# Forward table by a signed permutation on TensorE, last input part ahead of the inverse table, first filter copies on VectorE in finer parts

## The chip, the cores and the metric

The kernel runs on one core of one Trainium2 chip. The metric is the time of an execution on the device, in microseconds; lower is better. Each kernel was executed several times.

Engines are named as in the profile: PE is TensorE, PEld its weight loads, DVE is VectorE, ACT is ScalarE, POOL is GpSimd. The span runs from the first to the last instruction of the profiled execution; the device time of the same execution is about 2 us longer (792.0 against 793.8). An eviction is the copy by which another engine takes a matmul's result out of the bank that TensorE wrote it to, so that the bank is free again.

## The reference

The program filters a sequence in the frequency domain and applies a two-layer network with a Gelu to the result. Cut to what matters:

```
x: (8, 3008, 256)   filt_r, filt_i: (1505, 256)   w_in: (256, 2048)   w_out: (2048, 256)

X = rfft(x, axis=1)
y = irfft(X * (filt_r + 1j * filt_i), n=3008, axis=1)      # per batch and channel
h = y.reshape(24064, 256) @ w_in
out = (0.5 * h * (1 + erf(h / sqrt(2)))) @ w_out
```

## The kernel before

The transform of length 3008 = 47 x 64 is done by matmuls with tables in two steps each way. The tables are not read from memory: they are computed in the kernel (angles on VectorE, sines on ScalarE). Batch 0 runs ahead of the network in a stretch of its own; batches 1 to 7 are woven into the network's loop. Only the stretch of batch 0 is touched by the change. The second step works on 24 blocks, counted by `k`; each of its twelve products covers two of them. Its parts are:

- `c1`: 16 pieces of the first step on the input `x_sb`, evicted to `at_sb`.
- `table_2_angle`, `table_2_sin`: the forward table `T2` of the second step. `table_3`: the inverse table `T3`, which is `T2` transposed (24 transposes on TensorE). `table_4`: a small last table.
- `c1t`: transposes of `at_sb`. `c2`: the second step and the product with the filters `F`. `c3`, `c3t`, `c4`: the way back.
- `dup_filters`: partitions 64 to 127 of `F` are a copy of partitions 0 to 63.

```
    def dup_filters(self, eng, k0, k, ts=(0, 1)):
        for t in ts:
            o, i = (self.F[r:r + 64, t, k0:k0 + k, :].rearrange("p a b -> p (a b)") for r in (64, 0))
            ...
                eng.tensor_copy(out=o, in_=i)
    ...
    def table_2_sin(self, k0, k):
        act, t2 = self.nc.scalar.activation, self.T2[:, k0:k0 + k]
        w, r = self.gen[:, 0, k0:k0 + k], self.gen[:, 1, k0:k0 + k]
        act(out=t2[:, :, 1, :], in_=w, func=AF.Sin, scale=2.0 * PI)
        act(out=t2[:, :, 2, 0:32], in_=r[:, :, 0:32], func=AF.Sin, scale=-2.0 * PI, bias=self.hp)
        act(out=t2[:, :, 2, 32:64], in_=r[:, :, 32:64], func=AF.Sin, scale=2.0 * PI, bias=self.hm)
    ...
    for k, n in ((0, 4), (4, 6), (10, 6), (16, 8)):
        m.load_filters(k, n)
    m.load_w_in()
    for k, n in ((4, 6), (10, 6), (16, 4), (20, 4)):
        m.dup_filters(nc.gpsimd, k, n)

    for u in range(16):
        m.c1(u // 2, u % 2, False if 4 <= u < 8 or u % 2 and u > 7 else act)
        if u == 3:
            m.table_2_sin(0, 12)
        if u == 7:
            m.table_2_sin(12, 12)
            nc.scalar.activation(out=warm, in_=m.p, func=AF.Gelu)       # loads the Gelu table
            ...                                                         # T2[0] = -T2[2]; small copies T1p, T1q
        if u == 11:
            m.table_4()
            for q in range(3):
                m.table_3(q, act if q % 2 else False)
    ...
    m.c1t(0, False)
    m.c1t(1, act)
    m.dup_filters(nc.vector, 0, 4)
    for q in range(7):
        if q < 6:
            m.c2(2 * q)
            if q + 2 < 6:
                m.c1t(q + 2, act)
            m.c2(2 * q + 1)
        if q >= 1:
            m.c3(q - 1)
```

## Time and profile before

| | before |
|---|---|
| median time, us | 791.95 (790.87 to 792.96, 3 runs) |
| span of the profiled execution, us | 792.0 |
| PE busy over the span | 762.1 us, 96% |
| first `ps_h` matmul (first of the network's loop) | 50.17 us |
| first product `p` on VectorE | 25.42 us |

The busy share of PE is an average over two very different stretches. From the first `ps_h` matmul on, PE is busy nearly all the time. Before it (32.25 of the first 50 us busy), batch 0 is brought through a chain in which every engine waits for another in turn. The useful number for this change is therefore the start of the first `ps_h` matmul: everything ahead of it is what the change touches. The prediction shows the lines of this stretch and how to read them.

### The profile page before, as it was taken

The numbers are of one execution on the slowest core, as the hardware profiler recorded it, in microseconds if no ns is written. First come the engines' busy times: TensorE is split into PE (matmuls) and PEld (weight loads), VectorE is DVE, ScalarE is ACT, GpSimd is POOL, SyncE is SP. The second block draws the span as 40 slices with busy tenths as digits, with TensorE's granted clock in tenths as the row PEclk, the third lists the DMA queues.
The fourth block names the chain that finished last, engine by engine and source line by source line (L and its number), as shares of the span: only waits on it lengthen the run. The fifth ranks groups of instructions, "written<-read, shape, count | busy, mean of one in ns | idle before, by whom it ended". The sixth has DMA issues, their size and how long they took to land.

```text
span 792.0 us, 14572 instructions
## 1 busy us (share of the span) xinstructions
PE 762.1 (96%) x5817; PEld 539.9 (68%) x5914; DVE 411.2 (52%) x725; ACT 565.6 (71%) x963; POOL 64.7 (8%) x154
## 2 busy tenths in 40 slices
PE   4789999999999999999999999999999999999997
PEld 3666766677676767667677676666767777666666
DVE  7984756466464645646455564546645366421011
ACT  5578965798557885588755887569865688566663
POOL 8700200011000200002000020001100000000000
PEclk9999999999999999999999999999999999999999
DMA  9854862555435553446614566154642521501111
GB/s 142 152 93 131 159 159 67 147 119 112 115 84 156 104 133 84 111 138 130 144 50 107 146 123 157 38 162 107 124 130 63 164 76 60 133 28 40 41 41 54
DMA packets 86341, 85.64 MB, mean 108 GB/s; under 512 B 5824, under 2 KB 76480, under 8 KB 86272
## 3 DMA queue, kind: packets, MB, share of 16 engines
q1 hardware_dynamic: 77760, 68.70, 30.7%
q0 software_dynamic: 8512, 16.00, 14.2%
q8 instruction: 46, 0.75, 0.4%
q14 instruction: 23, 0.19, 0.1%
HBM read 54.00 MB, written 46.66 MB: 127 GB/s over the span
## 4 chain that ended last, share of the span: by engine, by line
PE 90%; DMA 3%; DVE 3%; ACT 1%; issue 1%; POOL 0%; SPq 0%; DVEq 0%; POOLq 0%
PE ps_o L436 40%; PE ps_h L422 37%; PE ps_s L240 3%; PE ps_s L313 3%; DMA d_sb<-R 3%; PE ps_s L263 2%; PE ps_s L288 2%; ACT y_sb L225 1%; PE ps_c L351 1%; PE ps_c L367 1%; DVE p L354 0%; DMA b_sb<-R 0%; DVE at_sb L227 0%; PE ps_t L216 0%; DVE F L99 0%
## 5 line engine op out<-in xcount | busy, mean ns | idle before, releaser
L425 ACT ACTIVATE g_sb<-ps_h 128x512 bf16<-128x512 f32 x752 | 439.2, 596 | 191.0 <-PE ps_h L422 163.2
L436 PE MATMUL ps_o<-w_out_sb,g_sb 128*128 128x256 bf16 x3008 | 449.1, 272 | 3.0
L422 PE MATMUL ps_h<-y_sb,w_in_sb 128*128 128x512 bf16 (+2 forms) x1503 | 426.6, 365 | 0.7 <-ACT y_sb L225 0.7
L436 PEld LDWEIGHTS <-g_sb 128*128 128x128 bf16 x3008 | 287.6, 98 | 133.8
L422 PEld LDWEIGHTS <-w_in_sb 128*128 128x128 bf16 x1600 | 155.0, 98 | 23.4 <-issue 0.9
L440 DVE COPY ost<-ps_o 128x512 f32<-128x512 f32 x94 | 64.3, 684 | 125.2 <-PE ps_o L436 124.7
L271 DVE TENSOR_TENSOR p<-ps_s,F 128x512 bf16<-128x512 f32 x84 | 58.1, 691 | 103.7 <-ACT p L270 97.1
L229 DVE TENSOR_SCALAR y_sb<-ps_s 128x376 bf16<-128x376 f32 x112 | 61.0, 548 | 83.5 <-PE ps_s L313 83.5
L227 DVE CAST a_sb<-ps_s 96x512 bf16<-96x512 f32 x112 | 76.3, 686 | 41.3 <-PE ps_s L240 41.2
L227 DVE CAST v_sb<-ps_s 128x512 bf16<-128x512 f32 x84 | 57.6, 686 | 13.0 <-PE ps_s L288 13.0
L269 ACT ACTIVATE p<-ps_s 64x512 bf16<-64x512 f32 x84 | 49.8, 593 | 2.0
L313 PEld LDWEIGHTS <-d_sb 96*128 96x128 bf16 x448 | 30.3, 97 | 29.7 <-DMA d_sb<-R 3.8
L270 ACT CAST p<-ps_s 64x512 bf16<-64x512 f32 x84 | 48.5, 577 | 1.0
L104 POOL COPY gate<-p 1x1 bf16<-1x1 bf16 x48 | 8.5, 177 | 490.1 <-DVE p L273 490.1
L240 PE MATMUL ps_s<-x_sb,T 94*96 94x512 bf16 x112 | 42.7, 381 | 0.5
L313 PE MATMUL ps_s<-T,d_sb 96*128 96x94 bf16 x448 | 36.3, 204 | 3.9 <-DMA d_sb<-R 2.7
L273 DVE TENSOR_TENSOR p<-p 128x512 bf16<-128x512 bf16 x84 | 35.7, 425 | 2.9
L272 DVE TENSOR_TENSOR p<-p,F 128x512 bf16<-128x512 bf16 x84 | 34.9, 415 | 0.0
L82 POOL DMA_DIRECT2D x_sb<-in_x_dram x64 | 32.5, 510 | 13.0 <-issue 11.0
L263 PE MATMUL ps_s<-b_sb,T 128*128 128x256 bf16 x168 | 32.1, 273 | 0.4
L288 PE MATMUL ps_s<-p,T 128*128 128x256 bf16 x168 | 32.1, 273 | 0.2
L288 PEld LDWEIGHTS <-T 128*128 128x128 bf16 x168 | 16.4, 98 | 20.0 <-DVE p L273 0.5
(91 smaller groups left out, 193.0 us busy)
## 6 DMA issues: line engine op xcount, KB each, us to landing
out_dram<-ost SPq DMA_DIRECT2D x94, 256.0 KB, 2.5
x_sb<-in_x_dram POOLq DMA_DIRECT2D x64, 188.0 KB, 3.9
R<-a_sb SPq DMA_DIRECT2D x56, 192.0 KB, 3.0
b_sb<-R SPq DMA_DIRECT2D x28, 384.0 KB, 4.3
R<-v_sb SPq DMA_DIRECT2D x42, 256.0 KB, 4.0
d_sb<-R SPq DMA_DIRECT2D x56, 192.0 KB, 4.5
w_in_sb<-in_moe_w_in_dram POOLq DMA_DIRECT2D x2, 512.0 KB, 8.7
w_out_sb<-in_moe_w_out_dram POOLq DMA_DIRECT2D x2, 512.0 KB, 10.9
```

Of the source, the lines that this page charges most:

```text
L227: self.nc.vector.tensor_copy(out=out, in_=in_)
L229: self.nc.vector.tensor_scalar(out=out, in0=in_, scalar1=scale, scalar2=None, op0=ALU.mult)
L240: nc.tensor.matmul(ps[0:96, :], lhsT=self.T1, rhs=self.st[b, "x"][:, 2 * u:2 * u + 2, :], start=True, stop=True)
L269: nc.scalar.activation(out=p2[0:64], in_=ps[64:128], func=AF.Copy, scale=-1.0)
L270: nc.scalar.copy(out=p2[64:128], in_=ps[0:64])
L271: nc.vector.tensor_tensor(out=p1, in0=ps, in1=f(0), op=ALU.mult)
L288: nc.tensor.matmul(ps[:, 256 * i:256 * i + 256], lhsT=self.T3[:, k].rearrange("p a b -> p (a b)"), rhs=w[:, 256 * i:256 * i + 256], start= ...
L313: nc.tensor.matmul(ps[:, 94 * i:94 * i + 94], lhsT=d[:, (grp % 2) * 4 + i, 128 * half:128 * half + 128], rhs=t4, start=True, stop=True)
L422: nc.tensor.matmul(ps[:, o:o + n], lhsT=self.w_in_sb[:, dc, jc * 128:jc * 128 + 128], rhs=self.ring[:, dc, off:off + n], start=(dc == 0), ...
L425: nc.scalar.activation(out=self.st["g", t][:, jc, :], in_=ps, func=AF.Gelu)
L436: nc.tensor.matmul(ps[:, tile_i % 2, :], lhsT=g[:, jc, tile_i * 128:tile_i * 128 + 128], rhs=self.w_out_sb[:, jc, :], start=(jc == 0), sto ...
L440: nc.vector.tensor_copy(out=ost, in_=ps)
```

## The change

The intent is to shorten the stretch before the first `ps_h` matmul in three ways, each meant to take work off VectorE's path:

1. **Rotated table.** The cosine part of `T2` is the sine part with pairs of rows exchanged and a sign. The change computes only sines and makes the rest by a matmul with a signed permutation matrix (`swap`), evicted by ScalarE. The second half's angles start from the first half's.
2. **Input ahead of the inverse table.** Only one third of `T3` is transposed before the last input part; the other two go into the product loop. `table_4` moves near the end of it, its small copies to GpSimd, its weights into a hole at the start. Evictions are shared out anew between VectorE and ScalarE, the Gelu table load moves into the product loop, and `c3` reads a product's tile in another order.
3. **Filter copies.** VectorE copies the first six `k` in three pieces of two `k` (both parts together) in place of four `k` in two pieces. GpSimd copies the next four ahead of the `w_in` load and the rest in pieces of two `k`.

The diff, cut to its core (cuts are marked with `...`):

```
-    def dup_filters(self, eng, k0, k, ts=(0, 1)):
-        for t in ts:
-            o, i = (self.F[r:r + 64, t, k0:k0 + k, :].rearrange("p a b -> p (a b)") for r in (64, 0))
...
+    def dup_filters(self, eng, k0, k):
+        for k in range(k0, k0 + k, 2):
+            o, i = (self.F[r:r + 64, :, k:k + 2, :].rearrange("p t a b -> p t (a b)") for r in (64, 0))
+            eng.tensor_copy(out=o, in_=i)
...
+        ts(out=self.swap, in0=cols, scalar1=self.to, scalar2=self.sg, op0=ALU.is_equal, op1=ALU.mult)
...
-        v.scalar_tensor_tensor(out=r, in0=w, scalar=-1.0, in1=w, op0=ALU.mult, op1=ALU.max)
...
-        act(out=t2[:, :, 2, 0:32], in_=r[:, :, 0:32], func=AF.Sin, scale=-2.0 * PI, bias=self.hp)
-        act(out=t2[:, :, 2, 32:64], in_=r[:, :, 32:64], func=AF.Sin, scale=2.0 * PI, bias=self.hm)
...
+    def table_2_swap(self, h):
+        t2 = self.T2[:, 12 * h:12 * h + 12]
+        for s, j in ((1.0, 0), (-1.0, 32)):
+            ps = self.bank("ps_sw", "n")
+            self.nc.tensor.matmul(ps[:, 0:384], lhsT=self.swap, rhs=t2[:, :, 1, j:j + 32], start=True, stop=True)
+            self._evac(t2[:, :, 2, j:j + 32], ps[:, 0:384].rearrange("p (k j) -> p k j", k=12), "act", s)
...
-    for k, n in ((0, 4), (4, 6), (10, 6), (16, 8)):
+    for k, n in ((0, 4), (4, 2), (6, 4), (10, 6), (16, 8)):
         m.load_filters(k, n)
+    m.dup_filters(nc.gpsimd, 6, 4)
     m.load_w_in()
-    for k, n in ((4, 6), (10, 6), (16, 4), (20, 4)):
-        m.dup_filters(nc.gpsimd, k, n)
+    ...                                     # T1p, T1q on GpSimd
+    m.dup_filters(nc.gpsimd, 10, 14)
...
-        m.c1(u // 2, u % 2, False if 4 <= u < 8 or u % 2 and u > 7 else act)
+        m.c1(u // 2, u % 2, act if u < 4 or u % 2 else False)
...
-            nc.scalar.activation(out=warm, in_=m.p, func=AF.Gelu)
...
         if u == 11:
-            m.table_4()
-            for q in range(3):
-                m.table_3(q, act if q % 2 else False)
+            m.table_3(0, False)
...
-    m.dup_filters(nc.vector, 0, 4)
+    m.dup_filters(nc.vector, 0, 6)
...
+        if 1 <= q < 3:
+            m.table_3(q, act)
+        if q == 3:
+            nc.scalar.activation(out=warm, in_=m.p, func=AF.Gelu)
         if q >= 1:
             m.c3(q - 1)
+        if q == 5:
+            m.table_4()
```

## The prediction

> **What bounds the kernel now.** The page puts PE at 96% busy, and ScalarE's and VectorE's shares at 71% and 52%. I asked next for the windows by stage: from 70 us on, PE is busy 29.79 of 30, 99.03 of 100, 197.13 of 200 us, so the long loop is bound by TensorE, and the diff touches nothing in it. What the diff touches lies before the first `ps_h` matmul, which the timeline has at 50.17 us. So the question is how many microseconds earlier that matmul comes; everything after is expected to shift as a block. I then read the chain that ended last, in order of time, from 5 to 27 us:
>
> ```profile
> 5.56 1.02 DVE gen L173
> ...
> 11.90 0.96 DVE gen L178
> 12.86 1.86 DVE at_sb L227 x4
> ...
> 16.34 2.73 PE ps_t L216 x24
> 19.09 1.22 DVE T L227
> 20.32 0.94 DVE at_sb L227 x2
> ...
> 22.63 2.70 DVE F L99 x2
> ...
> 25.42 1.24 DVE p L354
> ```
>
> The reader is to see that from 5.56 to 25.42 us the chain is nearly all VectorE: angles of the forward table, copies of the transformed input queued behind them, 24 transposes for the inverse table in the middle of PE's program, then two filter copies. After 25.42 the twelve products set the pace. The timeline shows this stage:
>
> ```profile
> 14.64 0.55 DVE L502 TENSOR_SCALAR T<-T 128x1536 bf16<-128x1536 bf16 x1
> 19.14 10.02 POOL L99 COPY F<-F 64x1536 bf16<-64x1536 bf16 x8
> 22.63 2.69 DVE L99 COPY F<-F 64x1024 bf16<-64x1024 bf16 x2
> 26.70 0.99 PE L351 MATMUL ps_c<-b_sb,T 128*128 128x256 bf16 x4 [2.57 <-DVE p L354]
> 27.48 1.06 PE L339 MATMUL ps_c1t<-eye,at_sb 128*128 128x128 bf16 x8
> 31.01 0.61 PE L339 MATMUL ps_c1t<-eye,at_sb 128*128 128x128 bf16 x8
> 31.21 9.14 DVE L354 TENSOR_TENSOR p<-ps_c,F 128x1024 bf16<-128x1024 f32 x8 [0.55 <-PE ps_c L351]
> ```
>
> Two things to see. The two filter copies of 1024 elements take 2.69 us together, while a larger copy-like VectorE operation (1536 elements, 128 partitions) takes 0.55: GpSimd was copying filters all that time. And PE, idle for 2.57 us before 26.70, then needs 1.06 us for eight transposes that take 0.61 at 31.01. The windows confirm the second:
>
> ```profile
> 25.00:26.00 1.00, 0.00 (x0) 1.00 1.04 209
> 27.00:28.00 1.00, 1.00 (x9) 0.50 0.07 12
> 31.00:32.00 1.00, 1.00 (x16) 1.00 1.01 184
> ```
>
> The fourth number is the granted clock: 1.00, then 0.50 after the idle stretch, 1.00 again by 31.
>
> **What the Trainium skill says.** "SBUF — State Buffer", section "Who interferes with whom": VectorE in a two-port mode and GpSimd share a port pair under an exclusive lock; the second to issue blocks for the whole instruction of the first. The trace agrees: VectorE's copies last 1.08 and 1.68 us, GpSimd's 64x1536 copies 1.34 us median with one stretched to 1.66, which is one VectorE copy (0.31 us) more. "VectorE: DVE Perf Modes", section "Side-by-side: where the cycles go for N=2048 bf16": four elements a cycle plus some 150 cycles at 0.96 GHz. For 1024 elements I estimate from this (256+150)/0.96 = 0.42 us; the same form gives 0.56 for 1536, and the trace has 0.55. "TensorE: Matmul & The Clock Gate", section "What's actually happening": half clock by default and after an idle window of about 3.4 us, full clock after a busy one. The trace agrees on the halving; its idle stretch was only 2.57 us, so here the threshold is at best approximate (the page's window is free-running).
>
> **The change part by part.** All starts below are worked from durations above and from rows of the same view.
>
> *Forward table.* Removed from VectorE: two absolute-value passes of 0.96 us, and the second half's angle starts from the first by a 0.56 us tensor-scalar in place of 1.02. Added: three one-column operations (about 0.2 us), one 128x128 mask (0.2). Removed from ScalarE: four sines of 128x384, 0.60 each. Added: four evictions of 128x384 at 0.49, and four matmuls of 384 columns, 0.5 us each at half clock. VectorE's angle work ends at about 5.76+1.02+0.58+0.98 (first half, 8.36), +0.4 (masks), +0.58+0.58+0.98 = 10.85, where it ended at 12.86. But the rotated quarter now goes sine, matmul, eviction: first sine 8.40 to 9.24, matmuls to 10.1, evictions to 10.7; second sine held behind input evictions until 11.9, done 12.76, matmuls 13.6, evictions 14.24, negation on VectorE 14.28 to 14.63. VectorE waits in that negation, so the two pieces of input meant for it go at 14.55 to 15.57. That gives back over half of the 2 us.
>
> *Input ahead of inverse tables.* In the order of PE's instructions, 8 transposes now stand before the last input part instead of 24 and two `ps_t4` matmuls: 16 x 0.107 + 0.36 = about 2.1 us off PE's stretch. One third is evicted on VectorE (1.22) at about 16.2 to 17.5; the last input part is evicted by 18.45 on both engines, where it was 21.26. The first transposes of it start at 18.5 instead of about 21.3 (-2.75 us), and VectorE reaches the filter copies at about 19.9 instead of 22.63. The other two thirds move into the product loop: 8 transposes (0.45) and a ScalarE eviction of 1.02 in each of two rounds.
>
> *Filter copies.* Three copies of 1024 instead of two. Alone: 3 x 0.33 = 1.0 us. GpSimd, however, now issues 20 filter loads instead of 16. It is held by input landings until the eighth is issued at 13.5; then 12 x 0.55 = 6.6 gives 20.1 us for its first copy. Against 19.9 for VectorE this is a close race. If VectorE wins, the first product starts at about 20.9 to 21; if it loses, each copy alternates with a 1.03 us GpSimd copy and the product starts at 23.0.
>
> *Products.* Twelve at a pace of 1.14 us (9.14 for eight), 13.7 us, plus gaps while PE catches up. In the good case PE idles only some 0.9 us before the third product's matmuls, so it keeps its clock; I count gaps of 0.2, 0.2 and 0.4 us around the rounds with the extra transposes. Last product ends 35.4 instead of 40.36: -5.0. In the bad case PE idles about 2.8 us, falls to half clock, and third to sixth product wait as they did: last end about 39.1, -1.2.
>
> *Rest.* GpSimd's later filter copies: two ready at 21.3 and 22.4, then w_in issues and two small copies, then seven from 24.0 to 31.4; product 5 needs the third at 26.9 and gets it at 25.1; product 8 has over 2 us in hand. The Gelu table load (1.28 + 0.20) moves from 14.03, where ScalarE was idle, to about 30.7, where the evictions of `vt` follow; the banks for the round after next are free again by 33.3 against a need at 33.6, so I count 0. The next input's load starts at 31.4 instead of 29.11 but is needed only after 44. The final stretch (8.1 us from 42.04 to 50.17) has the same operations. Sum: -5.0 to -1.2.
>
> **The rivals.** (a) *The copies lose the lock race*: speaks for it, that both sides come within 0.3 us by my sums; against, that a load being issued delays a copy little (the 0.55 above ran beside load issues) and the finer copies suit it. It makes 790.6. (b) *ScalarE becomes the bound of the product loop*: 1.02+1.02+2x0.55 = 3.1 us in a round with extra transposes against 2.28 for two products, plus the table load. Against: two such rounds only, three rounds of slack after. It would cost 0.5 to 1 us: 788. (c) *GpSimd's copies become the bound*: they end later than before (31.4 against 29.2) while products begin earlier. If load issues run 1.5 us longer than I count, each late product waits; 788.5. (d) *The shift is lost in the loop*, because later loads or the first DRAM round trip have less slack: loads have several us, so I give it little; then 791.
>
> **Range and chances.** I give the good case (-5, with (b) or (c) taking a little) about half, something in between (-3, one copy blocked) a quarter, the bad case (-1.3) a quarter: mean -3.6, and the three runs of before spread by 2 us. Prediction **788.2 us**, range **786.2 to 790.7**. 2% is 15.8 us; the whole stretch touched is 45 us and nothing in it can give that. Faster 0.01, same 0.985, slower 0.005.
>
> **What would show it.** First `ps_h` matmul at 45 to 49 us instead of 50.17. VectorE's angles end near 10.9; the first transposes of the whole input start near 18.5; three filter copies near 19.9, 0.3 to 0.4 us each if free and over 1 us if locked; the first product near 21 (23 if locked); granted clock 1.00 all through 20 to 30 us in the good case, 0.50 in the bad; products 1.14 us apart at the end. Wrong, if the second sine or the negation comes much later than 14.6 us, if the products wait for GpSimd, or if PE's busy share after the first `ps_h` falls.

## The result, and the profile after

The changed kernel took 789.82 us (median of 4 runs, 788.94 to 791.01) against 791.96 us of before (4 runs). The ratio is 0.9974, with a 95% interval of 0.9955 to 0.9994. Ratios are the mean time of one kernel's runs over that of the other's runs of the same rounds, so they are not quite the ratio of the medians quoted. Repeated later with more rounds, the ratio was 0.9964. By the rule of 2% it is the same time; as a small number it is 2.1 to 2.9 us faster. All outputs are right.

The first `ps_h` matmul now starts at 46.67 us, 3.50 us earlier. The chain that ended last, in order of time, in the part that was VectorE's before (start, length in us, what):

```profile
19.73 1.33 DVE F L96 x2
21.05 1.04 issue
22.10 0.42 DVE F L96
22.52 0.02 issue
22.54 0.03 DVE p L367
22.56 1.11 issue
23.68 1.23 DVE p L367
24.90 0.04 issue
24.95 0.60 PE ps_c L364 x4
25.54 0.45 PE ps_t L229 x8
25.99 0.89 PE ps_c L380 x16
```

The first product stands at 22.54 instead of 25.42. From about 25 us the chain is TensorE's: the transposes moved into the loop (`ps_t L229`) lie on it. The timeline of the same stretch:

```profile
17.93 1.89 PE L352 MATMUL ps_c1t<-eye,at_sb 128*128 128x128 bf16 x16 [0.55 <-DVE at_sb L240]
...
19.68 2.21 POOL L96 COPY F<-F 64x1024 bf16<-64x1024 bf16 x2
19.73 2.78 DVE L96 COPY F<-F 64x1024 bf16<-64x1024 bf16 x3
...
20.55 1.06 PE L352 MATMUL ps_c1t<-eye,at_sb 128*128 128x128 bf16 x8
...
23.82 0.61 PE L364 MATMUL ps_c<-b_sb,T 128*128 128x256 bf16 x4 [1.52 <-DVE p L367]
...
24.27 0.61 PE L352 MATMUL ps_c1t<-eye,at_sb 128*128 128x128 bf16 x8
...
27.82 9.14 DVE L367 TENSOR_TENSOR p<-ps_c,F 128x1024 bf16<-128x1024 f32 x8 [0.66 <-POOL F L96]
```

Three things are to be seen. GpSimd began its two filter copies at 19.68, and VectorE its three at 19.73: VectorE lost the race by 0.05 us, and its copies took 2.78 us. TensorE waited 1.52 us for the first product and was not slowed afterwards (eight transposes in 0.61 us at 24.27). But it ran at half speed before that: eight such transposes took 1.06 us at 20.55. The windows by microsecond, whose fourth number is the granted clock, do not show it:

```profile
20.00:21.00 1.00, 1.00 (x9) 1.00 0.99 140
...
25.00:26.00 1.00, 1.00 (x16) 1.00 1.08 217
...
27.00:28.00 1.00, 1.00 (x15) 1.00 1.06 213
```

The granted clock reads 1.00 at 20 us too. In the profile of early_copies (below) the same column reads 0.50 from 20 to 22 us, and eight transposes take 1.06 us there as well, so half clock is the likely reason here. In this early stretch the duration of an instruction, not that column, tells TensorE's speed.

In the last line of the timeline the wait of the fifth product is put down to a GpSimd copy. By the code this product reads `k` 8 and 9, which GpSimd's second copy fills, and that copy had ended at 21.89. What ends just before the product starts at 27.82 are TensorE's transposes (27.16 + 0.61 = 27.77). So the name is not to be trusted here; what held the product is not shown.

**After the first `ps_h` matmul.** The start was the same to 0.02 us in the two profiles of the changed kernel (46.67 and 46.69), and the time is not: it spreads by 2 us in either kernel. The waits of TensorE from 50.3 us to the end (total us, times, longest) show one source that repeats (left out is one wait of 0.7 us for ScalarE just after the start, in the kernel before). First the kernel before, then two profiles of the changed kernel:

```profile
PE ps_s L313 <- DMA d_sb<-R: 2.7, 6, 0.7
```

```profile
PE ps_s L326 <- DMA d_sb<-R: 0.6, 2, 0.3
PE ps_s L276 <- DMA b_sb<-R: 0.5, 1, 0.5
```

```profile
PE ps_s L326 <- DMA d_sb<-R: 2.1, 4, 0.6
PE ps_s L276 <- DMA b_sb<-R: 0.5, 1, 0.5
```

These are waits for the intermediate results of later batches on their way back from memory. Within one kernel they differ by 1.5 us (1.1 against 2.6), and the two spans differ by 1.1 us (787.2 and 788.3). This noise is as large as most effects studied below. So the experiments are judged by the first `ps_h` matmul, and the time is quoted beside it. This has a weakness: each kernel but the changed one has a single profile, and TensorE's speed in the start, which moves the first `ps_h`, is not the same in all of them (see early_copies and fine_unsplit).

### The profile page after: what moved, and what is told of

Same layout as the page of the kernel before. It is cut to its first block, busy times and chain, and to the rows that moved or that the text cites. A ratio compares the mean times of both kernels' runs of the same rounds, so it can differ in the third digit from the quotient of the medians.

```text
span 787.2 us, 14592 instructions
## 1 busy us (share of the span) xinstructions
PE 762.2 (97%) x5821; PEld 540.1 (69%) x5918; DVE 406.7 (52%) x720; ACT 567.4 (72%) x968; POOL 65.7 (8%) x161
## 4 chain that ended last, share of the span: by engine, by line
PE 93%; DMA 3%; issue 1%; POOL 1%; ACT 1%; DVE 1%; SPq 0%; DVEq 0%; POOLq 0%
PE ps_o L450 42%; PE ps_h L436 38%; PE ps_s L253 3%; PE ps_s L326 3%; PE ps_s L276 2%; PE ps_s L301 2%; DMA d_sb<-R 1%; DMA x_sb<-in_x_dram 1%; ACT y_sb L238 1%; PE ps_c L380 1%; POOL F L91 1%; PE ps_c L364 1%; DMA b_sb<-R 0%; POOL x_sb L82 0%; DMA F<-in_filt_i_dram 0%
## 5 line engine op out<-in xcount | busy, mean ns | idle before, releaser
L301 PEld LDWEIGHTS <-T 128*128 128x128 bf16 x168 | 16.4, 98 | 20.1 <-DVE p L286 0.5
```

The source lines that it names most:

```text
L301: nc.tensor.matmul(ps[:, 256 * i:256 * i + 256], lhsT=self.T3[:, k].rearrange("p a b -> p (a b)"), rhs=w[:, 256 * i:256 * i + 256], start= ...
```

## The experiments

Twelve runs were made, all with 5 rounds: the changed kernel again and eleven others. For each, the first `ps_h` matmul is from its one profile. The last column is span less first `ps_h` of that profile, which is the network's loop. By the rule of 2% every one of them is the same time as before. The intervals of the twelve ratios reach 0.0012 to 0.0016 to either side, about 1 us, so neighbours are not told apart by time.

| run | first product, us | first `ps_h`, us | median time, us | ratio to before | loop, us |
|---|---|---|---|---|---|
| before | 25.42 | 50.17 | 791.96 to 792.89 | 1 | 741.8 |
| after (result above) | 22.54 | 46.67 | 789.82 | 0.9974 | 740.5 |
| after_again | 22.55 | 46.69 | 789.99 | 0.9964 | 741.6 |
| early_copies | 20.97 | 45.69 | 788.18 | 0.9942 | 740.7 |
| undo_filters | 21.99 | 46.07 | 788.92 | 0.9950 | 741.7 |
| undo_table | 22.37 | 46.50 | 788.83 | 0.9951 | 741.7 |
| order_only | 20.58 | 45.25 | 787.46 | 0.9940 | 740.4 |
| undo_input | 22.86 | 46.24 | 788.84 | 0.9958 | 740.7 |
| early_warm | 20.88 | 45.59 | 787.55 | 0.9938 | 740.5 |
| before_small | 25.07 | 48.57 | 791.80 | 0.9995 | 740.7 |
| order_unsplit | 24.52 | 49.16 | 790.14 | 0.9965 | 740.2 |
| small_gelu | 24.62 | 48.11 | 790.29 | 0.9975 | 740.0 |
| order_warm | 20.61 | 45.24 | 788.15 | 0.9943 | 740.9 |
| fine_unsplit | 22.91 | 46.61 | 789.29 | 0.9966 | 741.0 |

The theory at the start was that VectorE's lost race for the ports had held the first product back, and that most of the gain comes from the order of TensorE's program. The main rivals were that the rotated table carries the gain, that TensorE's half clock bounds the stage, and that part of the gain is lost in the loop.

**after_again: the changed kernel once more.** No edit.

> The changed kernel once more, with more rounds. Both theories: first ps_h matmul at 46.7 us within 0.2, the three filter copies on VectorE about 1.25, 1.25 and 0.4 us. Theory 'the start's 3.5 us pass whole into the time': ratio to before 0.9956, about 788.5 us. Rival 'part of it is lost in the loop': ratio stays near 0.9974, and PE's busy share after the first ps_h matmul is lower than before's.

The start was the same to 0.02 us, and the ratio was 0.9964 (0.9951 to 0.9976). The mean difference is thus 0.0036 x 792.84 = 2.9 us, and the interval reaches to 3.9. The full 3.5 us is inside it, and so is a loss of over 1 us. In the first result's interval the same holds. The loop's length spreads by 1.8 us over the table, with no order by kernel that one profile each could show. Whether a little of the gain is lost in the loop stays open.

**early_copies: VectorE's filter copies moved into its wait.**

```
+    m.dup_filters(nc.vector, 0, 6)
     m.c1t(0, False)
     m.c1t(1, act)
-    m.dup_filters(nc.vector, 0, 6)
```

> The three first filter copies on VectorE stand before the first transposes' eviction, in the 1.1 us in which VectorE waited before 19.00. Theory 'the lock with GpSimd's copies delayed the first product': the copies take about 0.33 us apart between 17.9 and 19, the eviction stays at 19.0, the first product starts at about 20.8 instead of 22.54, the first ps_h matmul at about 45.0 instead of 46.7, time 1.7 us under the changed kernel's. Rival 'TensorE, still at half clock, is the bound after 19.7': first product at 20.8 too, but the gain shrinks to under 0.7 us by the first ps_h matmul. Rival 'GpSimd's later copies become the bound': products from the fourth on wait for GpSimd, same small gain.

The timeline of VectorE:

```profile
17.91 1.23 DVE L96 COPY F<-F 64x1024 bf16<-64x1024 bf16 x3
19.18 0.69 DVE L240 COPY b_sb<-ps_c1t 128x1024 bf16<-128x1024 bf16 x1
20.97 1.23 DVE L367 TENSOR_TENSOR p<-ps_c,F 128x1024 bf16<-128x1024 f32 x1 [1.10 <-PE ps_c L364]
22.68 3.48 DVE L367 TENSOR_TENSOR p<-ps_c,F 128x1024 bf16<-128x1024 f32 x3 [0.48 <-PE ps_c L364]
```

The three copies take 1.23 us together in place of 2.78, in a stretch in which GpSimd only issued filter loads. The lock theory (VectorE's copies are slow because GpSimd holds the ports that they share) holds for the first product, which is 1.57 us earlier (20.97 for 22.54). The first `ps_h` is earlier by only 1.00 us, between what the theory (1.7) and the rival of a TensorE bound (under 0.7) expected. Both waits in the lines are for TensorE (`ps_c L364`), so the rival has a part in it. At 788.18 us it is a little faster than both kernels: all of its runs lie below all of after_again's (at most 788.67 against at least 789.04).

One thing differs that the edit does not explain. The sixteen transposes of the whole input took 1.07 us here and 1.89 us in the changed kernel, and TensorE was quicker already at 15.48 us (twelve matmuls in 0.83 us against 1.17), while the first moved copy starts at 17.91. The first product did not come earlier by it: VectorE's eviction of these transposes began only when its copies were through, at 19.18 instead of 19.00.

**undo_filters: the third part undone.** The loads, GpSimd's copies and VectorE's two copies are as before; the small copies T1p and T1q stay on GpSimd.

```
-    for k, n in ((0, 4), (4, 2), (6, 4), (10, 6), (16, 8)):
+    for k, n in ((0, 4), (4, 6), (10, 6), (16, 8)):
-    m.dup_filters(nc.gpsimd, 6, 4)
-    m.dup_filters(nc.gpsimd, 10, 14)
+    for k, n in ((4, 6), (10, 6), (16, 4), (20, 4)):
+        m.dup_filters(nc.gpsimd, k, n)
-    m.dup_filters(nc.vector, 0, 6)
+    m.dup_filters(nc.vector, 0, 4)
```

> The changed kernel with the filter part undone: four loads groups, the old copies of one t each, two on VectorE. Theory 'the filter part gains nothing, since the race for the ports was lost either way': copies on VectorE together 1.6 to 2.7 us, first product at 22.0 to 22.9, first ps_h matmul within 0.4 us of 46.7. Rival 'the finer parts carry a good share': first product a microsecond later or more, first ps_h at 47.7 or later.

VectorE's two copies took 2.14 us, the first product came at 21.99, and the first `ps_h` at 46.07. The last is 0.2 us earlier than the theory's range: beside the other two parts, the filter part costs 0.60 us.

**undo_table: the first part undone.** The old sines, angles and constants are put back; the rest stays.

```
-            m.table_2_sin(0)
-            m.table_2_swap(0)
+            m.table_2_sin(0, 12)
...
-            m.table_2_minus(0)
-            m.table_2_sin(1)
-            m.table_2_swap(1)
-            m.table_2_minus(1)
+            m.table_2_sin(12, 12)
+            ...                             # T2[0] = -T2[2] for all 24 k, on VectorE
```

> The changed kernel with the forward table by sines again. Theory of the prediction, that the rotation gives back what it saves: VectorE's angles end at 12.9 instead of 10.9, but its negation comes at about 14.0 to 14.6 either way, the first transposes of the whole input at 17.9 within 0.4, first ps_h matmul 46.5 to 47.1. Rival 'the rotated table is the main source of the gain': first ps_h at 48.2 or later.

The first whole-input transposes start at 17.76 instead of 17.93, and the first `ps_h` at 46.50 instead of 46.67. The theory holds: the rotation is worth nothing here, though VectorE's angles end 2 us earlier with it (10.91 against 12.88). The reason shows in VectorE's negation, which waits for ScalarE either way (the changed kernel first, then undo_table):

```profile
14.07 0.49 DVE L199 TENSOR_SCALAR T<-T 128x768 bf16<-128x768 bf16 x1 [1.96 <-ACT T L238]
```

```profile
14.06 0.66 DVE L502 TENSOR_SCALAR T<-T 128x1536 bf16<-128x1536 bf16 x1 [0.26 <-ACT T L182]
```

The time saved on angles has become a wait: 1.96 us before the negation, where it was 0.26, and the negation starts at the same moment.

**order_only: parts one and three undone together.** What is left of the change is its second part. The edit is the two edits above.

> The changed kernel with both the rotated table and the filter part undone; what is left is the order: last input part ahead of two thirds of the inverse table, the small tables moved off VectorE, other engines for some evictions, the later table load. Theory 'the order alone carries the gain': first ps_h matmul at 45.8 to 46.4 us, at least as early as the changed kernel's 46.7; time ratio to before 0.994 to 0.996. Rival 'the three parts need one another, and undoing two of them loses what undoing one did not': first ps_h at 47.5 or later.

```profile
18.47 1.12 POOL L114 DMA_DIRECT2D w_in_sb<-in_moe_w_in_dram  x2
...
19.51 0.83 DVE L99 COPY F<-F 64x1024 bf16<-64x1024 bf16 x2
20.60 4.29 POOL L99 COPY F<-F 64x1536 bf16<-64x1536 bf16 x3
```

The first `ps_h` is at 45.25, even earlier than the theory's range, and the time is 787.46 us: 4.6 us under before, and the lowest of all. The lines of VectorE and GpSimd say why. VectorE comes to its copies at 19.51 while GpSimd is still busy with the `w_in` load and two small copies; both pieces take 0.83 us together. GpSimd's long copies start only at 20.60. The second part alone carries more than the whole gain. TensorE's half speed has a price in it too, but a limited one: the twelve products take 14.95 us from 20.58 on, against 13.67 us where they run without a gap (undo_input, below), so from the first product on it costs at most 1.28 us.

**undo_input: all of the inverse table ahead of the last input part again**, with parts one and three kept.

```
         if u == 11:
-            m.table_3(0, False)
+            for q in range(3):
+                m.table_3(q, act if q % 2 else False)
...
-        if 1 <= q < 3:
-            m.table_3(q, act)
```

> The changed kernel with all three thirds of the inverse table transposed ahead of the last input part, as in before; table 4 stays late. The prediction's step: 16 transposes at 0.107 us, 1.7 us, and their evictions return to the path, so the first transposes of the whole input start at about 19.7 instead of 17.9 and the first ps_h matmul at 48 or later. Rival 'the product loop gives it back': VectorE's filter copies then come after GpSimd's first two and run freely (0.4 us each), the first product starts at about 23 instead of 22.5, the two rounds lose 0.45 us each of transposes, and the first ps_h stays within 0.5 us of 46.7.

The transposes of the whole input start at 19.67 instead of 17.93, as the prediction's step has it, and yet the first `ps_h` comes 0.43 us earlier (46.24). The rival holds, though the copies are not free from the first: VectorE reaches them at 21.05, GpSimd's second copy ends at 21.75 (19.73 + 2.02), and VectorE's three take 1.78 us. The product loop then runs twelve products without a gap:

```profile
22.86 13.67 DVE L367 TENSOR_TENSOR p<-ps_c,F 128x1024 bf16<-128x1024 f32 x12
```

**order_unsplit: the same edit in the order-only kernel.**

> The order-only kernel with all 24 inverse-table transposes ahead of the last input part again. Beside the order-only kernel it prices the step 'last input part ahead of the inverse table' by itself. The prediction's step: 1.7 us of transposes come back to the path, first transposes of the whole input at 19.5 instead of 17.74, first ps_h matmul at 46.5 or later instead of 45.25. Rival 'the product loop gives back all of it' (as two of the rounds lose 0.45 us of transposes each, and the clock is up earlier): first ps_h within 0.4 us of 45.25.

The transposes start at 19.40 instead of 17.74, a step of 1.66 us, as expected. But the first `ps_h` comes at 49.16 instead of 45.25, 3.91 us later. The timeline:

```profile
19.66 4.48 POOL L99 COPY F<-F 64x1536 bf16<-64x1536 bf16 x3
21.22 3.20 DVE L99 COPY F<-F 64x1024 bf16<-64x1024 bf16 x2
...
25.80 0.61 PE L350 MATMUL ps_c<-b_sb,T 128*128 128x256 bf16 x4 [2.30 <-DVE p L353]
26.25 0.99 PE L338 MATMUL ps_c1t<-eye,at_sb 128*128 128x128 bf16 x8
```

VectorE arrives among GpSimd's long copies, and its two copies take 3.20 us where they took 0.83. With the 1.66 us this makes up the whole difference, which already stands at the first product (24.52 against 20.58). TensorE then waits 2.30 us, and its clock falls (0.50 granted from 27 to 28 us; the transposes at 26.25 take 0.99), as in the kernel before. That adds nothing against order_only, which had its half speed earlier: from the start of the first product to the end of the last, both take 14.9 us. By time the step is worth less than 3.91 us: the ratios are 0.9965 and 0.9940, some 2 us apart, and the profile of order_unsplit is that of its slowest run (791.15 us, the others 788.57 to 790.74).

**fine_unsplit: the filter part added to order_unsplit.** The edit is undo_filters backwards.

> The order-only kernel with the inverse table unsplit (which had its first ps_h at 49.16 us), and in addition the filter part of the change: finer copies, two of them on GpSimd ahead of the w_in load. Theory 'the filter part has a price when VectorE reaches its copies at 19.7 us and is worth 3 us when it reaches them at 21.2, because GpSimd is then past its first two copies and issuing loads': the three copies on VectorE take 1.0 to 1.8 us together instead of 3.20 for two, the first product starts at 22.4 to 23.1 instead of 24.52, TensorE's clock stays at 1.00 through 26 to 29 us, the first ps_h matmul comes at 46.0 to 46.6. Rival 'the rotated table, not the filter part, made the difference between 46.24 and 49.16': first ps_h at 48.5 or later.

The copies took 2.10 us, a little over the theory's range, since GpSimd began its two at 20.06. The first product came at 22.91, the clock read 1.00 from 25 to 29 us (but 0.50 from 22 to 24), and the first `ps_h` came at 46.61: 2.55 us earlier than in order_unsplit. Of these, 1.61 us stand at the first product; the rest comes in the product loop, in which order_unsplit had TensorE at half clock. So at the first `ps_h` the filter part gains when VectorE comes late and costs when it comes early, as the theory says. The time does not confirm the size: the ratios of the two kernels are 0.9966 and 0.9965, and their intervals (0.9954 to 0.9978 and 0.9951 to 0.9979) lie at most 2.0 us apart. The profiled run of order_unsplit was its slowest, so the 2.55 us may not be typical.

Together with the runs above, this gives the first `ps_h` (one profile each) for seven of the eight combinations of the three parts, where "split" is the inverse table split around the last input part and the small moves of the second part are kept in all:

| | not split | split |
|---|---|---|
| no other part | 49.16 | 45.25 |
| filter part | 46.61 | 46.50 |
| rotated table | not run | 46.07 |
| both | 46.24 | 46.67 |

**before_small: the kernel before with the small jobs alone moved.**

```
     m.table_1(g)
+    m.weights_4(g)
...
+    ...                                     # T1p, T1q on GpSimd after load_w_in
...
-            m.weights_4(g)
-            ...                             # T1p, T1q on VectorE
...
-            m.table_4()
+    ...                                     # table_4 after the fifth round, evicted on ScalarE
```

> The kernel before with the small jobs alone moved: the weights of table 4 computed early, its two small copies on GpSimd, table 4 late and evicted on ScalarE. Theory 'VectorE's and TensorE's path before the inverse table gets 1.0 us shorter by this and the rest follows': the inverse-table transposes start at about 15.3 instead of 16.34, the first product at about 24.4 instead of 25.4, the first ps_h at about 49.2 instead of 50.17. Rival 'the lock takes it back': first product at 25.2 or later, because the filter copies on VectorE still meet GpSimd's.

The inverse-table transposes start at 15.95, only 0.39 us earlier, and the first product at 25.07, so the first numbers of the theory fell. The first `ps_h` came at 48.57, 1.60 us earlier and more than expected, with TensorE's clock up after the wait this time (eight transposes in 0.61 us at 26.81). The time was 791.80, a ratio of 0.9995 (0.9979 to 1.001): the 1.6 us do not show in it beyond doubt. The chain says what took the place of the small jobs:

```profile
13.50 0.51 ACT T L185
14.01 0.02 issue
14.03 1.28 ACT L505
15.31 0.01 issue
15.32 0.20 ACT warm L505
15.52 0.39 ACT at_sb L224
15.91 0.04 issue
15.95 2.73 PE ps_t L215 x24
```

It is the Gelu table load (1.28 us) and its first use, on ScalarE, ahead of an eviction that frees a bank for TensorE.

**small_gelu: in addition the Gelu table load moved into the product loop.**

```
         if u == 7:
-            nc.scalar.activation(out=warm, in_=m.p, func=AF.Gelu)
...
+        if q == 3:
+            nc.scalar.activation(out=warm, in_=m.p, func=AF.Gelu)
```

> The kernel before with the small jobs moved, and in addition the Gelu table load moved into the product loop (after the sixth product's matmuls). Theory 'the table load, 1.28 + 0.20 us on ScalarE at 14 us, was the second gate of the inverse-table transposes, hidden behind the small jobs': these transposes start at 14.5 to 14.9 instead of 15.95, the first ps_h matmul at 47.1 to 47.6 instead of 48.57. Rival 'ScalarE had no part in it, as the prediction had it': both within 0.3 us of the kernel with the small jobs alone.

The transposes start at 15.08, 0.87 us earlier, and the first `ps_h` at 48.11, 0.46 us earlier. The table load was a gate, but a third one stood close behind it: TensorE's own matmuls on the third input part, which run from 13.42 to 15.27 just ahead of the transposes. Of the 0.87 us the lock took a part back: VectorE's two copies took 3.11 us where they took 2.73, and the first product came 0.45 us earlier.

**early_warm and order_warm: idle matmuls to bring TensorE's clock up.** Matmuls with an unused result were put into TensorE's waits, 34 beside the early copies and 44 in the order-only kernel.

```
+    def busy(n):
+        ps = m.bank("ps_busy", "w")
+        for i in range(n):
+            nc.tensor.matmul(ps[0:96, 0, 0:96], lhsT=m.T1c, rhs=m.T1c, start=True, stop=True)
...
         if u == 3:
+            busy(20)
...
         if u == 7:
+            busy(14)
```

> The early filter copies, and in addition 34 idle matmuls on TensorE in its two waits near 7.5 and 11.3 us, so that its clock is up by the time the last input part comes (their result is not used). Theory 'half clock between 18 and 23 us kept the early copies' gain at 1.0 us instead of 1.7': eight transposes take 0.6 us instead of 1.07 at 18 us, the first product starts at about 20.5, the second at 21.7 instead of 22.7, the first ps_h matmul at 44.7 to 45.0 instead of 45.7. Rival 'the gain was lost to TensorE's amount of work in the rounds with extra transposes': first ps_h at 45.5 or later.

> The order-only kernel with 44 idle matmuls in TensorE's four waits between 7.2 and 17.7 us, the last 6 just ahead of the whole input's transposes, so that TensorE is busy without a break from about 13.4 us on. Theory 'half clock from 17.7 to 22.9 us costs 1 to 1.5 us': 16 transposes at 17.7 take about 1.0 us instead of 1.86, the third product starts at 22.2 instead of 23.4, the first ps_h matmul at 43.8 to 44.4 instead of 45.25, and the time is a microsecond under the order-only kernel's. Rival 'VectorE is the bound of this stage anyway': transposes faster, first ps_h at 45.0 or later. If the 16 transposes still take 1.8 us, or the clock falls again before 22 us, the run says nothing on it.

Neither settled the question. In early_warm the clock was up at 17.95 us and fell again:

```profile
17.95 1.07 PE L352 MATMUL ps_c1t<-eye,at_sb 128*128 128x128 bf16 x16 [0.82 <-DVE at_sb L240]
19.83 1.01 PE L364 MATMUL ps_c<-b_sb,T 128*128 128x256 bf16 x4 [0.81 <-DVE b_sb L240]
20.63 1.06 PE L352 MATMUL ps_c1t<-eye,at_sb 128*128 128x128 bf16 x8
...
23.00 0.61 PE L352 MATMUL ps_c1t<-eye,at_sb 128*128 128x128 bf16 x8
```

Sixteen transposes in 1.07 us at 17.95 are full speed; eight in 1.06 us at 20.63 are half speed; at 23.00 it is full again. The idle matmuls did not bring this about: early_copies, without them, has the same sixteen in 1.07 us, the same fall and the same rise. (The expectation took its 1.07 us for eight transposes at half speed; it was sixteen at full speed.) The first `ps_h` came 0.10 us earlier than in early_copies. In order_warm the sixteen transposes took 1.86 us as without the idle matmuls, and the first `ps_h` was unchanged (45.24), so by its own words that run says nothing. What half speed from 18 to 23 us costs stays open, within the bound given under order_only. By ratio, early_warm (0.9938), order_only (0.9940), early_copies and order_warm are not told apart.

## Why the prediction was right, and where its steps were not

The time of 789.82 us lies within 786.2 to 790.7, and the forecast of a small gain was right. The point, 788.2, asked for 1.6 us more than the first median gave (791.95 less the mean of 3.6 would have been 788.35).

- **The whole question lies before the first `ps_h`, and the rest shifts as a block.** Right for the start, which moved by 3.50 us. That this is so close to the expected mean of 3.6 is luck: the mean is that of three cases, -5.0, -3 (one copy blocked) and -1.3 (race lost). VectorE lost the race, two of its three copies were blocked, and yet the start came 2.3 us earlier than in the bad case. Most of that lies in the twelve products, where the half clock expected after the wait did not come. The block's own length varies by more than a microsecond through waits for read-back transfers (1.1 and 2.6 us in two profiles of one kernel). That this, and not a loss caused by the change, hides part of the gain was not shown.
- **"That gives back over half of the 2 us"** (rotated table). Right in kind, too small: undo_table shows that all of it is given back. Angles ended at 10.91 and the negation started at 14.07, against 10.85 (its own terms add up to 10.90) and 14.28 in the prediction. The old table has its negation at 14.06.
- **"about 2.1 us off PE's stretch"** (input ahead of the inverse table). The transposes of the input moved as worked out: 17.93 measured against 18.5. The pure step measured 1.66 us (17.74 against 19.40). What failed is taking the step's worth from the length of the transposes: at the first `ps_h` it is worth 3.91 us without the other parts (some 2 us by the ratios) and -0.43 us with both.
- **The race for the ports.** The prediction put VectorE at 19.9 and GpSimd at 20.1 and gave the good case about half. Measured were 19.73 and 19.68, so the race was lost as in rival (a), with the first product at 22.54 against 23.0 for that case. It was named as a close race, and early_copies, order_only and fine_unsplit confirm the mechanism. What was missed is the size of the lock's part in the kernel before, and that it makes the parts depend on one another. Two readings under it were off. A free copy was counted as 0.33 us and measured 0.41 (1.23 for three). And the median of 1.34 us for GpSimd's 64x1536 copies is taken over four of these and four of 64x1024; the first three of 64x1536 took about 1.45 us each, so the one of 1.66 was stretched by 0.2 us, not by a whole VectorE copy.
- **"In the bad case PE idles about 2.8 us, falls to half clock"** failed. PE idled 1.52 us and ran at full speed afterwards. The matmuls from 18 to 22 us ran at half speed, which the prediction did not have; they ended only at 22.30, and so the wait was short. Why the speed then was full is not shown.
- **"the twelve products set the pace"** held: they took 14.42 us from 22.54 on, where the good case had 13.7 and gaps of 0.8, with one gap of 0.66 us. From 25 to 32 us the chain that ended last names TensorE, with the moved transposes on it; TensorE had no slack there, and yet VectorE lost little. The last product ended at 27.82 + 9.14 = 36.96, between the 35.4 and 39.1 of the two cases. The term that was mis-sized is this stage in the bad case: 16.1 us (39.1 less 23.0) against 14.42. Of the 3.50 us, 2.88 stand at the first product and 0.51 come in this stage (14.93 us before).
- **The Gelu table load "where ScalarE was idle", counted as 0.** Wrong for its old place: before_small shows it on the chain, and small_gelu measures 0.46 us at the first `ps_h` for moving it, in that kernel.
- **Rivals (b) and (c).** In the changed kernel no product was held by GpSimd's later copies, as far as the trace shows; in order_warm the third product waited 0.15 us for one (it ended at 23.64, the product starts at 23.67). ScalarE held TensorE back once in the product loop, by 0.37 us near 36.8 us, in the changed kernel.

So the kernel gains mainly by its order, and the parts do not add up: at the first `ps_h` of one profile each, the split alone brings 3.91 us, the filter part alone 2.55, both together 2.66 (49.16 less 46.50), and all three 2.49 (49.16 less 46.67). By these profiles, two parts of the change cost more than they bring beside the third. Undoing both gives the lowest median measured, 787.46 us, and a ratio whose interval (0.9927 to 0.9952) only just meets that of after_again (0.9951 to 0.9976).

## What to carry to other kernels

When two engines share a lock, the worth of any step ahead of it depends on which one arrives first: find both arrival times in the timeline, and if they lie within the error of the estimate, move one of them out of the way rather than guess. Before cutting work on one engine, look at what the next consumer waits for besides it, since here 2 us of saved angles became a 1.96 us wait. When the whole time is noisier than the effect, judge experiments by a fixed event in the trace that repeats (here to 0.02 us in two profiles), take more than one profile of each kernel, since one may be of an unusual run, and test the parts in combinations, because undoing parts one by one from the full change gave numbers that did not add.

## What the Trainium skill lacked or had wrong

- "TensorE: Matmul & The Clock Gate", section "What's actually happening", gives half clock after an idle window of about 3.4 us, with a free-running window. The runs show that the length of a wait does not tell when the clock falls: the clock fell after TensorE waits of 2.57 us (before) and 2.30 us (order_unsplit), not after one of 2.99 us (small_gelu, eight transposes in 0.61 us right after it), and in early_warm it fell (0.50 granted from 20 to 22 us) with no wait above 0.82 us from 17.95 us on. Nor did 44 idle matmuls raise it in order_warm (sixteen transposes in 1.86 us with them and without). The section's window does not foresee this in a start with many short waits.
- "SBUF — State Buffer", section "Who interferes with whom", is confirmed: VectorE copies of 64x1024 take about 0.41 us each when free (1.23 us for three) and up to 1.6 us each on average (3.20 for two) among GpSimd's 64x1536 copies. What it does not say is that the losses come again with every copy, since the two engines take turns (in the changed kernel, VectorE's first two copies end 1.27 and 2.45 us after the first began, the third takes 0.41 once GpSimd is through). Beside finer pieces of 64x1024 three copies took 1.78 to 2.78 us.
- "ScalarE: Activation LUTs", section "What ACT_TABLE_LOAD costs", gives some 1283 ns for the load and some 1380 ns of drain with it. The load agrees (1.28 us); no drain of that length shows: in before_small the sine before it ends at 14.01, the load takes 1.28 us from 14.03, and the first Gelu starts at 15.32.
- Beyond a general warning, on the page on TensorE, that clock events in a trace can be unreliable, no page says that the granted clock can read 1.00 while TensorE runs at half speed early in a kernel (1.00 from 20 to 21 us, with eight transposes in 1.06 us in place of 0.61).
